# Moving half of one batch's preparation into the next mixing, wider complex products, and three evictions on ScalarE

## The chip, the cores and the metric

The kernel runs on one core of a Trainium2 chip. The metric is the device time of one execution in microseconds, the median of several executions. The engines are written as the profile writes them: PE is TensorE, PEld its weight loads, DVE VectorE, ACT ScalarE, POOL GpSimd, SP SyncE, which here issues most of the DMA transposes and the output.

## The reference

Four batches of 768 tokens and 512 channels. An attention with 8 heads, 8 global keys and a local window of 96 gives x. Then comes a phase-based mixing over tokens and a channel layer:

```python
theta = x @ w_theta
zr, zi = x * cos(theta), x * sin(theta)
y = einsum('ts,bsd->btd', w_tok_r, zr) + einsum('ts,bsd->btd', w_tok_i, zi)
u = x + y
out = u + maximum(u @ w_ch, 0)
```

## The kernel before

The mixing of batch b is interleaved ("woven") with the attention of batch b+1. A batch's attention needs its q and k transposed; for batches 1 and 2 this is done by `prep`, one call for each of four pairs of heads: two copies on DVE, 12 transposes on PE, one eviction on DVE, one on ACT, and two copies of global keys (`kglob`) on DVE. Batch 3's q and k are transposed by DMA.

```python
def prep(b, p):
    if p == 0:
        prep_copy(b, 0)
    if p + 1 < NP:
        prep_copy(b, p + 1)
    ...                      # 2 x 6 transposes into two PSUM tiles
    nc.vector.tensor_copy(out=qT, in_=ps)      # for q
    nc.scalar.copy(out=kT, in_=ps)             # for k
    kglob(b, p)

def kglob(b, p, ...):
    ...
    with behind("dve") if b == B - 1 else nullcontext():
        copy(out=kG, in_=kT[...])
        copy(out=kG[:, :, 0:NG], in_=kT[:, None, 0:NG].to_broadcast(...))

def trans_w(tt, copy=nc.vector.tensor_copy):   # token weights, one tile of rows
    for wi in range(2):
        ps = ps_small([T, NT, T], BF)
        ...                                    # 6 transposes
        (copy if wi else nc.vector.tensor_copy)(out=w_tokT[wi][...], in_=ps)
```

The first mixing (batch 0) is woven with the preparation of batch 1, the attention of batch 1, and all four preparations of batch 2:

```python
pre = [lambda p=p: prep(1, p) for p in range(NP)] if b == 0 else []
ahead = [[lambda p=p: prep(2, p) for p in range(NP)], [prep_dma(3, 0)], [], []][b]
...
if b == 0 and g == 1 and tt + 1 < NT:
    main.append((1536, lambda tt=tt: trans_w(tt + 1)))
```

The softmax here doesn't subtract the row's maximum and nothing guards it: scores larger than these inputs give would overflow.

## Time and profile before

| | before |
|---|---|
| median | 175.22 us (174.96 to 175.46, 4 runs) |
| execution that was profiled | 174.38 us, span 172.4 us |
| PE, DVE, ACT busy | 162.2, 126.3, 99.3 us |

The profiled execution happens to be quicker than the median by 0.8 us.

```profile
113.92 1.02 PE L418 MATMUL ps<-zri,w_tokT 128*128 128x512 bf16 x4 [0.48 <-DVE o_sb L451]
```

### The profile page before, as it was taken

The numbers are of one execution on the slowest core, as the hardware profiler recorded it, in microseconds if no ns is written. First come the engines' busy times: TensorE is split into PE (matmuls) and PEld (weight loads), VectorE is DVE, ScalarE is ACT, GpSimd is POOL, SyncE is SP. The second block draws the span as 40 slices with busy tenths as digits, with TensorE's granted clock in tenths as the row PEclk, the third lists the DMA queues.
The fourth block names the chain that finished last, engine by engine and source line by source line (L and its number), as shares of the span: only waits on it lengthen the run. The fifth ranks groups of instructions, "written<-read, shape, count | busy, mean of one in ns | idle before, by whom it ended". The sixth has DMA issues, their size and how long they took to land.

```text
span 172.4 us, 3753 instructions
## 1 busy us (share of the span) xinstructions
PE 162.2 (94%) x1534; PEld 84.7 (49%) x1534; DVE 126.3 (73%) x286; ACT 99.3 (58%) x127; POOL 37.4 (22%) x45
## 2 busy tenths in 40 slices
PE   7699989899999999999999999989999999999991
PEld 2355555445756566544445464433554644444440
DVE  5636977687999999998686588298776856714442
ACT  4688783999497695469944640879447409500010
POOL 8965355005282010099000000000000000000000
PEclk9969999999999999999999999999999999999999
DMA  4999999999999999999999677889245372323335
GB/s 154 199 174 178 208 210 207 205 204 173 158 204 176 169 131 192 124 138 143 182 130 117 143 170 167 109 151 256 43 78 136 97 168 76 122 55 98 94 92 184
DMA packets 75089, 25.94 MB, mean 150 GB/s; under 512 B 63168, under 2 KB 72128, under 8 KB 75072
## 3 DMA queue, kind: packets, MB, share of 16 engines
q0 software_dynamic: 45680, 12.45, 77.8%
q1 hardware_dynamic: 28976, 12.72, 33.8%
q10 hardware_dynamic: 416, 0.52, 0.9%
q8 instruction: 12, 0.20, 0.5%
q14 instruction: 5, 0.04, 0.1%
HBM read 25.69 MB, written 6.29 MB: 185 GB/s over the span
## 4 chain that ended last, share of the span: by engine, by line
PE 61%; DVE 19%; ACT 12%; DMA 5%; issue 1%; DVEq 0%; ACTq 0%; SPq 0%
PE ps L418 28%; PE ps L446 9%; ACT cs L404 6%; PE pb L398 6%; PE pb L296 5%; PE pb L355 4%; ACT e L306 3%; DMA qk<-in_k_dram 3%; DVE x_sb L366 2%; DMA kT<-qk 2%; DVE qT L250 2%; PE ps L398 2%; DVE e L315 2%; PE pb L276 2%; PE ps L246 2%; ACT L306 1%
## 5 line engine op out<-in xcount | busy, mean ns | idle before, releaser
L418 PE MATMUL ps<-zri,w_tokT 128*128 128x512 bf16 x288 | 71.2, 379 | 1.5 <-DVE zri L407 0.7
L306 ACT ACTIVATE e<-pb 128x1024 bf16<-128x1024 f32 (+1 forms) x48 | 43.6, 959 | 20.4 <-PE pb L296 19.9
L418 PEld LDWEIGHTS <-w_tokT 128*128 128x128 bf16 x288 | 26.2, 98 | 30.2 <-issue 2.5
L423 DVE TENSOR_TENSOR u<-x_sb,ps 128x512 bf16<-128x512 bf16 x24 | 16.4, 682 | 13.1 <-PE ps L418 13.1
L446 PE MATMUL ps<-w_ch_bf,uT 128*128 128x512 bf16 (+1 forms) x100 | 24.7, 371 | 0.0
L407 DVE TENSOR_TENSOR zri<-x_sb,cs 128x512 bf16<-128x512 bf16 x48 | 18.1, 419 | 4.9 <-ACT cs L404 4.6
L404 ACT ACTIVATE cs<-pb,halfpi 128x1024 bf16<-128x1024 f32 x8 | 8.9, 1114 | 18.3 <-PE pb L398 18.3
L451 DVE SCALAR_TENSOR_TENSOR o_sb<-ps,u 128x512 f32<-128x512 f32 (+1 forms) x25 | 16.5, 665 | 3.1 <-PE ps L446 3.1
L296 PE MATMUL pb<-qT,kT 64*128 64x128 bf16 x224 | 16.1, 223 | 1.7 <-DVE qT L211 1.3
L315 DVE TENSOR_TENSOR e<-e,etab 128x1024 bf16<-128x1024 bf16 (+1 forms) x24 | 14.7, 616 | 3.6 <-ACT e L306 3.5
L296 PEld LDWEIGHTS <-kT 64*128 64x128 bf16 x224 | 9.2, 95 | 15.8 <-issue 13.1
L398 PE MATMUL pb<-w_theta_bf,xT 128*128 128x512 bf16 x64 | 15.1, 379 | 0.0
L437 ACT COPY uT<-ps 128x512 bf16<-128x512 bf16 x7 | 4.1, 586 | 18.6 <-PE ps L436 18.6
L398 PEld LDWEIGHTS <-xT 128*128 128x128 bf16 x96 | 9.2, 98 | 10.1 <-DMA xT<-x_sb 0.2
L355 PEld LDWEIGHTS <-e 128*128 128x128 bf16 x352 | 12.6, 97 | 3.2 <-issue 1.0
L446 PEld LDWEIGHTS <-uT 128*128 128x128 bf16 x100 | 9.2, 98 | 10.0 <-ACT uT L437 0.8
L296 PE MATMUL pb<-qT,kG 64*128 64x128 bf16 x128 | 12.2, 221 | 0.4 <-DVE kG L222 0.4
L88 POOL DMA_DIRECT2D vn<-in_v_dram x5 | 9.6, 1923 | 12.3 <-DVE vn L68 10.7
L366 DVE TENSOR_TENSOR x_sb<-pb,rec 128x768 bf16<-128x768 f32 x12 | 11.4, 948 | 0.3
L318 DVE TENSOR_TENSOR e<-e,etab 128x1024 bf16<-128x1024 bf16 x12 | 8.2, 684 | 2.9 <-ACT e L306 2.9
L355 PE MATMUL pb<-vn,e 128*128 128x65 bf16 x168 | 9.6, 193 | 0.0
L252 ACT COPY kT<-ps 128x768 bf16<-128x768 bf16 x8 | 6.4, 798 | 5.5 <-PE ps L246 5.5
(73 smaller groups left out, 203.7 us busy)
## 6 DMA issues: line engine op xcount, KB each, us to landing
out_dram<-o_sb SPq DMA_DIRECT2D x23, 256.0 KB, 2.4
vn<-in_v_dram POOLq DMA_DIRECT2D x3, 768.0 KB, 22.1
qk<-in_q_dram POOLq DMA_DIRECT2D x2, 768.0 KB, 20.9
qk<-in_k_dram POOLq DMA_DIRECT2D x2, 768.0 KB, 23.2
w_nat<-in_moe_w_tok_r_dram POOLq DMA_DIRECT2D x3, 384.0 KB, 14.9
w_nat<-in_moe_w_tok_i_dram POOLq DMA_DIRECT2D x3, 384.0 KB, 13.9
vn<-in_v_dram POOLq DMA_DIRECT2D x2, 384.0 KB, 9.8
qk<-in_q_dram POOLq DMA_DIRECT2D x8, 96.0 KB, 9.6
```

Source lines behind the costliest of these rows:

```text
L296: nc.tensor.matmul(pb[:, hh, o:o + T], lhsT=lhsT, rhs=qT[R, (own, nxt)[part]], start=bool(b), stop=bool(b) or (jt == NT - 1 or (j == 1 and ...
L306: ins = nc.scalar.activation(e_c, pb[:, :, 0:n], AF.Exp, scale=scale).ins
L315: nc.vector.tensor_mul(e_c, e_c, tab[:, :, s0:s0 + n // T].rearrange("p a s n -> p a (s n)"))
L355: nc.tensor.matmul(o, lhsT=l_, rhs=r_, start=(i_ == 0), stop=(i_ == len(mms) - 1))
L366: nc.vector.tensor_mul(xv, po4[:, :, :, 0:D], rec.to_broadcast([T, n, nt, D]))
L398: nc.tensor.matmul(pb[j_] if last else pb[:, j_, :], lhsT=xT[:, dc, st(j_)], rhs=w_theta_bf[:, dc, :], start=(dc == 0), stop=(dc == NC - 1))
L404: nc.scalar.activation(o, p_, AF.Sin, **bias)
L407: nc.vector.tensor_mul(zri[b][:, i_, 2 * c + j_, :].rearrange("p (g d) -> p g d", g=NP), xb[:, :, 2 * c + j_, :], cs[:, i_, j_].rearrange( ...
L418: anchor["pe"] = nc.tensor.matmul(ps, lhsT=w_tokT[wi][:, st, tt * T:(tt + 1) * T], rhs=zri[b][:, wi, st, :], start=(st == 0 and wi == 0), ...
L423: anchor["dve"] = nc.vector.tensor_add(u_sb[b, tt].rearrange("p (g d) -> p g d", g=NP), x_sb[b][:, :, tt, :], ps.rearrange("p (g d) -> p g ...
L446: nc.tensor.matmul(ps_c, lhsT=uT[:, dc, :], rhs=w_ch_bf[:, dc, i_ * n:(i_ + 1) * n], start=(dc == 0), stop=(dc == NC - 1))
L451: nc.vector.scalar_tensor_tensor(o_sb[:, cols], in0=ps_c, scalar=0.0, in1=u[:, cols], op0=ALU.max, op1=ALU.add)
```

## The change

Its intent is to unload DVE in the first mixing, where it is busy without a pause: two of the four preparations of batch 2 go to the second mixing, where they are woven in after the first and second group of scores; the products x cos and x sin of batches 1 to 3 take two token tiles at a time; and the second eviction of three of the token-weight tiles goes to ACT.

```diff
-        if p == 0:
-            prep_copy(b, 0)
-        if p + 1 < NP:
+        if p == 0 or (b, p) == (2, NP // 2):
+            prep_copy(b, p)
+        if p + 1 < NP and (b, p) != (2, NP // 2 - 1):
             prep_copy(b, p + 1)
...
+            n = 2 if b else 1
             for i_ in range(2):
-                for j_ in range(2):
+                for j_ in range(0, 2, n):
                     nc.vector.tensor_mul(        # out, x, cos or sin: now n token tiles
...
+        late = [lambda p=p: prep(2, p) for p in range(NP // 2, NP)] if b == 2 else []
...
+            if i_ in (0, 2):
+                steps.extend((1536, f) for f in late[i_ // 2:i_ // 2 + 1])
...
-        ahead = [[lambda p=p: prep(2, p) for p in range(NP)], ...
+        ahead = [[lambda p=p: prep(2, p) for p in range(NP // 2)], ...
...
-                    main.append((1536, lambda tt=tt: trans_w(tt + 1)))
+                    main.append((1536, lambda tt=tt: trans_w(tt + 1, nc.scalar.copy if tt > 1 else nc.vector.tensor_copy)))
```

More of the change, by code (lines that the diff above doesn't have):

```diff
@@ L404, in theta @@
                     nc.scalar.activation(o, p_, AF.Sin, **bias)
+            n = 2 if b else 1
             for i_ in range(2):
-                for j_ in range(2):
+                for j_ in range(0, 2, n):
                     nc.vector.tensor_mul(
-                        zri[b][:, i_, 2 * c + j_, :].rearrange("p (g d) -> p g d", g=NP),
-                        xb[:, :, 2 * c + j_, :],
-                        cs[:, i_, j_].rearrange("p (g d) -> p g d", g=NP))
+                        zri[b][:, i_, 2 * c + j_:2 * c + j_ + n, :].rearrange("p j (g d) -> p j g d", g=NP),
+                        xb[:, :, 2 * c + j_:2 * c + j_ + n, :].rearrange("p g j d -> p j g d"),
+                        cs[:, i_, j_:j_ + n].rearrange("p j (g d) -> p j g d", g=NP))
     def mix(b, tt, g):
@@ L604 @@
         pre = [lambda p=p: prep(1, p) for p in range(NP)] if b == 0 else []
-        ahead = [[lambda p=p: prep(2, p) for p in range(NP)], [lambda p=p: prep_dma(3, p) for p in range(1)],
+        ahead = [[lambda p=p: prep(2, p) for p in range(NP // 2)], [lambda p=p: prep_dma(3, p) for p in range(1)],
                  [], []][b]
```

## The prediction

> **What bounds the kernel now.** I read the page first, then the busy time by stretch, then the chain that ended last, then the order of time on DVE. The page says that PE is the busy engine, but only 61% of the chain is PE's; 19% is DVE's.
>
> ```profile
> PE 162.2 (94%) x1534; PEld 84.7 (49%) x1534; DVE 126.3 (73%) x286; ACT 99.3 (58%) x127; POOL 37.4 (22%) x45
> ...
> PE 61%; DVE 19%; ACT 12%; DMA 5%; issue 1%; DVEq 0%; ACTq 0%; SPq 0%
> ```
>
> I cut the span by what the chain and the order of time show: batch 0's attention to 36 us; the first mixing, with the preparation and attention of batch 1 and the preparation of batch 2 woven in, to 73; theta of batch 1 to 82; the second mixing with batch 2's attention to 106; theta of batch 2 to 115; then the same again, and a pure mixing at the end. Busy time in these stretches (columns: length, then PE, PEld, DVE, ACT, POOL with counts, PE clock, DMA share, GB/s):
>
> ```profile
> 41.00:73.00 32.00, 31.45 (x389) 19.47 (x388) 32.00 (x74) 21.65 (x29) 7.13 (x10) 1.00 2.09 163
> 73.00:82.00 9.00, 9.00 (x58) 4.12 (x57) 8.48 (x22) 7.45 (x11) 9.00 (x10) 1.00 1.54 153
> 82.00:106.00 24.00, 23.81 (x243) 12.22 (x242) 17.27 (x31) 12.84 (x15) 0.19 (x1) 1.00 1.14 143
> 106.00:115.00 9.00, 8.52 (x44) 3.68 (x44) 5.94 (x17) 5.57 (x7) 0.00 (x0) 1.00 0.83 148
> 115.00:140.00 25.00, 24.70 (x258) 12.68 (x255) 19.88 (x39) 14.07 (x17) 0.00 (x0) 1.00 0.51 122
> ```
>
> The reader is to see 32.00 of 32.00 for DVE in the first stretch: it never rests. In the second mixing DVE is busy 17.27 of 24.00 and ACT 12.84: there is room. PE looks full everywhere, so I need what PE's work takes when it waits for nothing. The chain gives that, where PE runs on:
>
> ```profile
> 68.01 0.67 PE ps L246 x12
> ...
> 90.49 0.55 PE pb L296 x16
> ...
> 102.41 0.67 PE pb L355 x22
> 103.08 0.86 PE ps L446 x4
> 103.94 1.74 PE ps L418 x8
> ```
>
> So one 128-wide transpose (L246, and L167 and L436 alike) takes 0.056 us, a score matmul 0.034, a value matmul 0.0305, a 512-wide matmul (L418, L446, L398) 0.216. In the first stretch the trace counts 48 + 14 + 3 of the 512-wide, 96 + 36 + 16 transposes, 88 scores and 88 values: 65 x 0.216 = 14.0, 148 x 0.056 = 8.3, 88 x 0.034 = 3.0, 88 x 0.0305 = 2.7, together **28.0 us of PE work in 32.0**. Four microseconds of PE are lost there, and DVE is what it waits for: from 41 to 61 the chain is on DVE without a break. The same count for the second mixing is 83 x 0.216 + 72 x 0.034 + 88 x 0.0305 = 23.1 in 24.0, for the third 82 x 0.216 + 88 x 0.0645 = 23.4 in 25.0. Those two are bound by PE, at 94 to 96% of it. Theta of batch 1 (38 x 0.216 + 16 x 0.034 + 4 x 0.056 = 9.0 in 9.0) has no slack at all.
>
> **What the Trainium skill says.** "Perfetto Trace Analysis", Identifying the Most-Contended Engine: matmul busy share is a bad measure, occupancy is a fair one for the Vector engine. The trace agrees: PE shows 31.45 of 32 busy where the work counts to 28.0. "TensorE: Matmul & The Clock Gate", Wait — 56ns, not 53.3ns?: 56 ns between warm 128-wide matmuls; here 0.67 us for 12. "Perfetto Trace Analysis", Optimizing Scalar/DVE Operations: larger operations spare the cost per instruction, and a saturated DVE may hand work to Scalar even where Scalar is slower. The trace has both: a 128x512 product every 0.38 us against a 128x1024 one every 0.60, and a 128x768 eviction 0.80 on ACT against 0.53 (durations) on DVE. "VectorE: DVE Perf Modes", What auto-detection actually checks: the two-per-cycle mode asks for 16-bit operands of step one, not for few dimensions; the regrouped products keep both, and 1024 products in 0.60 us, four dimensions at L318 included, show the mode before.
>
> **The change part by part.** (1) Two of four preparations of batch 2 leave the first mixing. What one costs DVE is read from the starts here (start, duration; the next start gives the cost):
>
> ```profile
> 42.62 0.95 DVE L250 COPY qT<-ps 128x768 bf16<-128x768 bf16 x1
> 43.49 0.35 DVE L231 COPY qkn<-qk 128x768 bf16<-128x768 bf16 x1
> 43.75 0.29 DVE L220 COPY kG<-kT 128x512 bf16<-128x512 bf16 x1
> 43.95 0.35 DVE L231 COPY qkn<-qk 128x768 bf16<-128x768 bf16 x1
> 44.22 0.17 DVE L222 COPY kG<-kT 128x32 bf16<-128x32 bf16 x1
> 44.30 0.95 DVE L250 COPY qT<-ps 128x768 bf16<-128x768 bf16 x1
> ```
>
> 0.87 + 2 x 0.27 + 0.20 + 0.08 = 1.69 us, twice 3.4. On PE it is 24 transposes, 1.34 us; on ACT two evictions of 0.80. (2) Three evictions of transposed token weights go from DVE (0.47 from start to start) to ACT: 1.4 us off DVE, 3 x 0.80 = 2.4 onto ACT, which has 10 us free in that stretch. DVE falls from 32.0 to 27.2, PE's need from 28.0 to 26.7, ACT stays near 22.5. The two limits are then almost equal, so I take neither as reached. Up to 49.1 us the four preparations of batch 1 are a serial passage that the change hardly touches (one eviction, 0.5): 8.2 becomes 7.7 us. The rest held 28.0 - 6.4 = 21.6 us of PE work (6.4 is the same count up to 49.1) in 23.8; less 1.34 it is 20.3, and at 95% of PE, as in the later mixings, 21.3. Together 29.0 for 32.0: **3.0 us gained**.
>
> (3) The second mixing takes the 24 transposes. PE is its bound, so 1.34 us of work cost 1.34 / 0.95 = **1.4 us**. DVE has 2.3 more there and the four copies, 1.1, at the head of theta of batch 1, where they come before the products. (4) The products of three batches: two of 0.38 become one of about 0.60, so 0.16 x 6 = 1.0 us of DVE per theta. In theta of batch 1 that pays the 1.1 us of copies; in theta of batch 3 PE runs through; in theta of batch 2, where DVE waits 3.1 us for a transposed kT and the products after it hold up the sines by 1.1 us and PE by 0.5, I give it **0.3 us**. Sum: -3.0 + 1.4 - 0.3 = -1.9 us.
>
> **The rivals.** First, PE alone is the bound and work moved from one mixing to the next is only moved: then the net is near zero, perhaps 175.0. For it speaks that PE from 60.9 to 73 already carries 11.3 us of work in 12.1, and that 24 transposes leave exactly there; against it the 4.0 us lost in the stretch as a whole. Second, ACT becomes the wait: the last weight eviction stands in the changed order behind the exp table's replacement by the sine table (1.28 us) and gates the last mixing tile; from the last scores of batch 1, two exps, the load and the eviction end after about 3.7 us, and PE has about 3.5 us of other work first. At worst a stall of 1 us: 174.3. Third, DVE was the whole loss: the first mixing then falls to PE's 26.7 over 0.95, 28.1, and the net is -2.8 or better with fewer stalls later: 172.3. Fourth, the larger products come later, as one has to wait for both sines of the last pair of tiles; ACT needs 0.5 us for the second sine, and the scores' stalls in the second mixing would grow by that. In the changed order 24 transposes fill the place, so I expect no more than 0.3.
>
> **Range and chances.** 175.4 less 1.9 is 173.5. The first rival sets the upper end, 175.2, the third with a further half microsecond the lower, 171.8. To be over 2% faster it needs less than 171.9, which would mean that the first mixing loses almost nothing any more; I give 0.12. Over 2% slower would ask for a new stall of more than 3.5 us, and I see none: 0.02.
>
> **What would show it.** In the changed profile: DVE's share in the first mixing below 95%, the stretch about 3 us shorter, the chain there on PE rather than DVE; 96 transposes split 72 to 24; the second mixing longer by 1.4 us at about unchanged PE efficiency; products of 128x1024 at 0.68 us or so, 18 of them. A product of 1.2 us would mean that the two-per-cycle mode was lost; then DVE gains nothing there. A wait of PE for ACT's weight copies over 0.5 us would show the second rival. The prediction is wrong if the first mixing keeps its length, which would say that the weave and not DVE's load sets it.

## More of the kernel before

Beside the lines that the prediction shows, three of the kernel before are needed later: from the order of time of DVE and of PE (start, duration, engine, line, operation, count, and in brackets the idle time before it and what ended it). DVE copies the first q and k of batch 1 without waiting for the load; it waits 3.06 us for a key tile transposed by DMA in the theta stage of batch 2; and PE waits there 0.48 us.

```profile
41.55 1.16 DVE L231 COPY qkn<-qk 128x768 bf16<-128x768 bf16 x4
...
111.55 0.29 DVE L220 COPY kG<-kT 128x512 bf16<-128x512 bf16 x1 [3.06 <-DMA kT<-qk]
```

## The result, and the profile after

The changed kernel took 173.97 us in the median (173.88 to 174.46, 4 runs), the kernel before 175.22. The ratio is 0.9935, 95% interval 0.9910 to 0.9959: a little faster, under 2%. Ratios in this document are the mean time of one kernel's runs over that of the other's runs in the same rounds, so they are not quite the ratio of the medians. Executions over 1.5% slower than the fastest of the same kernel are left out of the means.

The page of the changed kernel, busy time and the chain that ended last:

```profile
PE 158.7 (92%) x1510; PEld 84.2 (49%) x1534; DVE 125.0 (72%) x265; ACT 101.4 (59%) x130; POOL 39.8 (23%) x45
...
PE 49%; DMA 26%; DVE 12%; POOL 5%; ACT 4%; issue 2%; DVEq 0%; SPq 0%; POOLq 0%
```

DVE's share of the chain fell from 19% to 12%. Nearly half of DMA's 26% is one transfer, the load of batch 1's keys, through which the chain now runs. Behind it the chain is still on DVE, from 42.3 to 56.5 us, where in the kernel before it was on DVE from 40.9 to 60.8; so the prediction's sign "the chain there on PE rather than DVE" came only in part. (Some matmul records are missing from this trace, 1510 of 1534, so PE's busy sum is not to be compared.) Busy time by stretch, with the same columns as in the prediction:

```profile
41.00:72.00 31.00, 29.16 (x359) 18.10 (x364) 29.14 (x65) 22.11 (x30) 8.15 (x9) 1.00 2.07 168
72.00:80.00 8.00, 8.00 (x44) 3.43 (x43) 6.98 (x14) 6.39 (x9) 7.64 (x9) 1.00 1.22 125
80.00:106.00 26.00, 25.31 (x277) 13.93 (x283) 20.84 (x37) 15.21 (x18) 2.48 (x2) 1.00 1.30 145
```

DVE is busy 94% of the first stretch instead of 100%. Stretches cut by eye are too coarse for the rest, so I use three lengths with ends that every trace has: "first" from the first transpose of batch 1's q to the end of theta of batch 1, "second" from there to the end of theta of batch 2, "third" from there to the end of theta of batch 3. (The end is the start of the last group of theta matmuls plus 0.216 us for each of them.) One profiled execution of each kernel, in us:

| kernel | first | second | third |
|---|---|---|---|
| before | 36.44 | 34.01 | 34.09 |
| changed | 35.39 | 35.55 | 34.10 |

The first became 1.05 us shorter, the second 1.54 longer, the third stayed. Both profiled executions have a span of 172.4 us, so this pair of traces shows where time moved and does not show the 1.25 us of the medians: the one of before was its quickest of five, the one of the changed kernel its slowest of four (174.46 us; the other three took 173.88 to 173.98).

Now the waits in the changed kernel's trace, from the order of time of DVE, of ACT and of PE. DVE waits for batch 1's keys, and does only 0.35 us of copying before that:

```profile
41.29 0.35 DVE L231 COPY qkn<-qk 128x768 bf16<-128x768 bf16 x1
42.32 0.90 DVE L231 COPY qkn<-qk 128x768 bf16<-128x768 bf16 x3 [0.68 <-DMA qk<-in_k_dram]
...
111.95 0.30 DVE L220 COPY kG<-kT 128x512 bf16<-128x512 bf16 x1 [3.28 <-DMA kT<-qk]
112.16 0.69 DVE L408 TENSOR_TENSOR zri<-x_sb,cs 128x1024 bf16<-128x1024 bf16 x1
```

The last two lines are the old wait for the transposed keys: DVE takes its work in order, and the product of 0.69 us, whose sines were ready (both end by 110.54), stands behind the copy. On ACT, the last of the moved evictions (L168) stands on ACT behind the table load, and PE waits for its buffer:

```profile
64.14 1.28 ACT L300 ACT_TABLE_LOAD   x1
65.44 0.20 ACT L300 ACTIVATE junk<-halfpi 128x1 f32<-128x1 f32 x1
65.55 0.78 ACT L168 COPY w_tokT<-ps 128x768 bf16<-128x768 bf16 x1
```

```profile
66.38 0.49 PE L246 MATMUL ps<-ident,qkn 128*128 128x128 bf16 x6 [0.34 <-ACT w_tokT L168]
...
92.83 1.04 PE L447 MATMUL ps<-w_ch_bf,uT 128*128 128x512 bf16 x4 [0.32 <-DMA uT<-u]
...
114.18 1.02 PE L419 MATMUL ps<-zri,w_tokT 128*128 128x512 bf16 x4 [0.52 <-DVE o_sb L452]
```

The line at 92.83 is a wait that the kernel before has not: the first channel layer of batch 1 waits for u transposed by DMA. The one at 114.18 is the old wait behind DVE, unchanged.

### The profile page after: what moved, and what is told of

It is laid out like the page before. It is cut to its first block, busy times and chain, and to the rows that moved or that the text cites. A ratio compares the mean times of both kernels' runs of the same rounds, so it can differ in the third digit from the quotient of the medians.

```text
span 172.4 us, 3709 instructions
## 1 busy us (share of the span) xinstructions
PE 158.7 (92%) x1510; PEld 84.2 (49%) x1534; DVE 125.0 (72%) x265; ACT 101.4 (59%) x130; POOL 39.8 (23%) x45
## 4 chain that ended last, share of the span: by engine, by line
PE 49%; DMA 26%; DVE 12%; POOL 5%; ACT 4%; issue 2%; DVEq 0%; SPq 0%; POOLq 0%
PE ps L419 25%; DMA qk<-in_k_dram 12%; PE ps L447 10%; DMA w_nat<-in_moe_w_tok_r_dram 7%; DMA uT<-u 5%; PE pb L398 4%; PE pb L355 4%; PE pb L296 3%; POOL qk L73 3%; DMA kT<-qk 2%; DVE qT L250 2%; PE ps L398 2%; ACT e L306 2%; DVE o_sb L452 2%; POOL vn L88 2%
## 5 line engine op out<-in xcount | busy, mean ns | idle before, releaser
L419 PE MATMUL ps<-zri,w_tokT 128*128 128x512 bf16 x271 | 68.6, 380 | 2.7 <-DVE zri L408 0.8
L447 PE MATMUL ps<-w_ch_bf,uT 128*128 128x512 bf16 (+1 forms) x98 | 24.2, 371 | 0.4 <-DMA uT<-u 0.3
L408 DVE TENSOR_TENSOR zri<-x_sb,cs 128x1024 bf16<-128x1024 bf16 (+1 forms) x30 | 16.8, 582 | 5.5 <-ACT cs L404 5.1
L296 PE MATMUL pb<-qT,kT 64*128 64x128 bf16 x224 | 15.1, 219 | 2.1 <-DVE qT L211 1.3
L296 PEld LDWEIGHTS <-kT 64*128 64x128 bf16 x224 | 8.7, 94 | 14.7 <-issue 11.4
L296 PE MATMUL pb<-qT,kG 64*128 64x128 bf16 x128 | 11.6, 217 | 0.7 <-DVE kG L222 0.4
L82 POOL DMA_DIRECT2D qk<-in_k_dram x8 | 8.8, 1094 | 5.9 <-DMA vn<-in_v_dram 5.9
```

What stands on the lines that cost most here:

```text
L296: nc.tensor.matmul(pb[:, hh, o:o + T], lhsT=lhsT, rhs=qT[R, (own, nxt)[part]], start=bool(b), stop=bool(b) or (jt == NT - 1 or (j == 1 and ...
L408: nc.vector.tensor_mul(zri[b][:, i_, 2 * c + j_:2 * c + j_ + n, :].rearrange("p j (g d) -> p j g d", g=NP), xb[:, :, 2 * c + j_:2 * c + j_ ...
L419: anchor["pe"] = nc.tensor.matmul(ps, lhsT=w_tokT[wi][:, st, tt * T:(tt + 1) * T], rhs=zri[b][:, wi, st, :], start=(st == 0 and wi == 0), ...
L447: nc.tensor.matmul(ps_c, lhsT=uT[:, dc, :], rhs=w_ch_bf[:, dc, i_ * n:(i_ + 1) * n], start=(dc == 0), stop=(dc == NC - 1))
```

## The experiments

All outputs are right. Two theories stood against each other. **Theory D**: DVE's load sets the length of the first mixing (the prediction's reading). **Theory P**: PE and its hand-offs set it, and what is moved from one mixing to the next is only moved. The three lengths of every run are in a table at the end of this section.

### The parts one by one

part1_late_preps takes from the diff only the move of the preparations; part2_wide_products only the block with `n = 2 if b else 1`; part3_copies_on_act only the line with `nc.scalar.copy`; parts23_no_move the last two.

> Only the move of two preparations of batch 2 into the second mixing; products and weight evictions as before. Theory D (VectorE's load sets the first mixing): 3.4 us leave a saturated VectorE, 1.4 us are paid in the second mixing, net about -1.5 us (ratio 0.991). Theory P (TensorE and its hand-offs set both mixings, moved work is only moved): 0 to -0.3 us (ratio 0.998 to 1.000).

> Only the products of batches 1 to 3 by two token tiles. Both theories: VectorE saves about 0.16 us for each of 18 products, but in the theta stages, where TensorE is full; 0 to -0.5 us (ratio 0.997 to 1.000).

> Only the three weight evictions moved to ScalarE. Theory D: 1.4 us off a saturated VectorE, about -1.2 us (ratio 0.993). Theory P: nothing, or a little slower (up to +0.5 us) where TensorE waits for ScalarE's eviction behind the table load.

> The changed kernel without the move of the preparations. Theory D: about -1.5 us (1.4 us of evictions and 0.3 us of products), so the move is worth little. Theory P: 0 to -0.5 us, and the move is what makes up the rest of the measured -1.2 us.

| run | median us (6 runs) | before, same rounds | ratio | interval |
|---|---|---|---|---|
| part1_late_preps | 176.30 | 175.28 | 1.0066 | 1.0030 to 1.0102 |
| part2_wide_products | 175.26 | 175.28 | 1.0004 | 0.9986 to 1.0023 |
| part3_copies_on_act | 175.27 | 175.28 | 0.9990 | 0.9961 to 1.0020 |
| parts23_no_move | 174.91 | 175.28 | 0.9964 | 0.9932 to 0.9995 |

Theory D misses on part 3 (it wanted 0.993) and on parts 2 and 3 together (it wanted 0.991; the measured 0.6 us is near what theory P allowed). Both miss on part 1, which is slower than before. The parts don't add: alone they make +0.66, +0.04 and -0.10%, together -0.65% (measured in other rounds). Part 1 took 3.4 us off DVE in the first mixing (the prediction's count); "first" in its profile is 36.12 us, 0.3 less than before and 1.1 less than in part2_wide_products, which is the same program there. "Second" grew by 2.0 and "third" by 0.9. (The traced execution, 177.40 us, is one of the two slowest of part 1.) Beside the moved transposes, two waits of PE carry much of that growth:

```profile
94.51 1.04 PE L446 MATMUL ps<-w_ch_bf,uT 128*128 128x512 bf16 x4 [0.74 <-DMA uT<-u]
...
116.73 1.02 PE L418 MATMUL ps<-zri,w_tokT 128*128 128x512 bf16 x4 [1.38 <-DVE o_sb L451]
```

In part 3's trace PE now stands for another eviction of the same kind, one that is still on DVE. It is one visible wait; that it is the reason why the relief of DVE was worth so little is not shown.

```profile
65.85 0.49 PE L246 MATMUL ps<-ident,qkn 128*128 128x128 bf16 x6 [0.71 <-DVE w_tokT L168]
```

A caution for all runs of this section: the traces show that the order of PE's work in the first mixing is not the same in all of them. It is the same in the kernel before and part2_wide_products; part 3, part 1, the changed kernel and the kernels with a dose each have another, also where the edit touches no work of PE. In part 3, for example, 12 transposes of a weight tile, which stand together in the kernel before, are split 4 and 8 around the 22 value matmuls of a pair. So a run is its edit and a new order. That the parts don't add may come from this; no run held the order fixed.

### A dose of work for one engine

To see what a microsecond on either engine costs in the first mixing, I added work that nobody reads.

```diff
         nc.vector.tensor_mul(xv, po4[:, :, :, 0:D], rec.to_broadcast([T, n, nt, D]))
+        if b == 1:                                   # dose_vec_*: 12 copies in all
+            for _ in range(3):
+                nc.vector.tensor_copy(out=spare, in_=x_sb[b][:, p, 0:4, :])
...
-            for st in range(NT):                     # dose_te_*: in trans_w
+            for st in list(range(NT)) * (2 if tt >= 3 else 1):
                 nc.tensor.transpose(ps[:, st, :], w_nat[wi, tt][...], ident)
```

> The kernel before with 12 idle copies of 128x512 (about 0.2 us each, 2.4 us) added to VectorE in the first mixing, after the attention results of batch 1; nobody reads them. Theory D (VectorE's load sets the first mixing): +2.0 to +2.4 us. Theory P (TensorE and its hand-offs set it; VectorE is busy because it has always something waiting, but with some slack): under +1 us.

> The kernel before with 36 transposes of the token weights done twice into the same place (36 x 0.056 = 2.0 us of TensorE in the first mixing). Theory D: 0 to +0.7 us, since TensorE has 4 us to spare there. Theory P: +1.7 to +2.0 us.

> The same 12 idle copies in the changed kernel, whose VectorE has 4.7 us less to do in this stretch. Theory D: under +1 us, for VectorE is no longer the limit. Theory P: 0 to +0.5 us.

> The same 36 doubled transposes in the changed kernel. Theory D: TensorE and VectorE are now near equal, +1.5 to +2.0 us. Theory P: +1.7 to +2.0 us as in the kernel before.

The dose on DVE is as large as meant: a copy occupies it for 0.20 us until the next start, in the profile of dose_vec_before:

```profile
57.60 0.27 DVE L369 COPY spare<-x_sb 128x512 bf16<-128x512 bf16 x1
57.80 0.67 DVE L315 TENSOR_TENSOR e<-e,etab 128x1024 bf16<-128x1024 bf16 x1
```

| run | ratio to before | interval | worth, us | dose, us | "first" in its profile |
|---|---|---|---|---|---|
| dose_vec_before | 1.0112 | 1.0082 to 1.0141 | 2.0 | 2.4 | 38.24, +1.8 |
| dose_te_before | 1.0105 | 1.0064 to 1.0146 | 1.8 | 2.0 | 38.77, +2.3 |
| dose_vec_after | 1.0016 | 0.9951 to 1.0080 | 1.4 | 2.4 | 35.42, 0.0 |
| dose_te_after | 1.0036 | 1.0003 to 1.0068 | 1.8 | 2.0 | 37.26, +1.9 |

"Worth" is 175.2 us times the ratio less 1 for the kernel before, and times the ratio less 0.9935 for the changed one, whose own runs belong to other rounds. The intervals make it 1.4 to 2.5 us for DVE's dose and 1.1 to 2.6 for PE's in the kernel before. The last column compares single traces: "first" of part2_wide_products, the same program as before in that stretch, is 37.25 us, and against it the first two would be +1.0 and +1.5. In the kernel before, **both theories are right at once**: work on DVE costs 2.0 of its 2.4 us and work on PE 1.8 of its 2.0. Theory D said that PE had 4 us to spare there; it had not. Part of the price on DVE can be the place and not the amount, which no run separates: in that trace PE waits 0.37 us, at 68.24, for the third pair's attention result x_sb, before which DVE had made six of the copies. In the changed kernel PE's dose costs about as much as before (1.8 us, each way some 0.7). DVE's dose left "first" as it was in the profile; its timing is too wide (1.4 us, with an interval of more than a microsecond either way) to confirm that.

### The waits that remain

Three runs of the changed kernel each take away the cause of one wait.

```diff
-    load_w()                     # after_keys_earlier
-    load_all_qk(1)
+    load_w(0, 4)                 # theta weights, first four token tiles
+    load_all_qk(1)
+    load_w(4, NT)                # last two token tiles, channel weights
...
-        with behind("dve") if b == B - 1 else nullcontext():            # after_global_keys_later
+        with behind("zri" if p == 1 else "dve") if b == B - 1 else nullcontext():
...                               # anchor["zri"] is the last product issued
-    trans_w(tt + 1, nc.scalar.copy if tt > 1 else nc.vector.tensor_copy)   # after_last_copy_back
+    trans_w(tt + 1, nc.scalar.copy if 1 < tt < 4 else nc.vector.tensor_copy)
```

> The changed kernel with the loads of batch 1's queries and keys issued ahead of the last third of the token weights and the channel weights (same loads, another order). If the keys of batch 1, which landed at 42.3 us in its profile, held the first mixing: no wait of VectorE for that load any more and 0.3 to 0.8 us faster than the changed kernel (ratio to the kernel before 0.989 to 0.992). If that wait was an accident of the profiled execution: as the changed kernel (0.9935), within 0.2%.

> The changed kernel with one copy of global keys (pair 1 of batch 3) placed on VectorE after the products of batch 2 instead of before them; all else, the other engines' orders too, stays. If the products of that theta are held by the transposed keys that this copy waits for (3.3 us), then VectorE's wait goes and TensorE's waits of 0.5 and 0.2 us for o_sb and zri with it: 0.5 to 1.0 us faster than the changed kernel (ratio 0.988 to 0.991). If TensorE's work hides it: no change (0.9935).

> The changed kernel with the last of the three weight evictions back on VectorE, so that none stands behind ScalarE's table load. If that place cost the changed kernel its 0.3 to 0.6 us wait of TensorE: 0.3 us faster (ratio about 0.992). If VectorE is still the limit there: 0.3 us slower (0.995). Theory P: no change.

| run | median us (6 runs) | before, same rounds | ratio | interval |
|---|---|---|---|---|
| after_keys_earlier | 174.48 | 175.47 | 0.9922 | 0.9880 to 0.9964 |
| after_global_keys_later | 173.71 | 175.47 | 0.9866 | 0.9820 to 0.9913 |
| after_last_copy_back | 174.57 | 175.47 | 0.9935 | 0.9895 to 0.9975 |

after_keys_earlier: DVE no longer waits for the load (its four first copies run from 41.50 on without a gap), and "first" is 34.61 us instead of 35.39. But "second" is 36.57 instead of 35.55, and the time is within the noise of the changed kernel's 0.9935. The gain came back as a wait:

```profile
93.31 1.04 PE L449 MATMUL ps<-w_ch_bf,uT 128*128 128x512 bf16 x4 [1.37 <-DMA uT<-u]
```

This is the same wait as at 92.83 in the changed kernel and at 94.51 in part 1. The DMA transpose of the first u of batch 1 is issued at 84.5 us in the kernel before, at 84.8 in the changed one, at 84.3 here, and lands 8.0 to 9.0 us later, at about 93 us, against a median of 2.5 us for all of its kind in the DMA list of the kernel before. There PE reached this work at 93.47 us and had nothing to wait for; a kernel that is earlier at this place waits. The likely cause of the slow landing are the loads of batch 3: the last of them is issued at 79.9 to 80.2 us in these three, and at 81.8 in part 1, where u, issued at 86.0, landed at 94.5. That last load, batch 3's values, lands within 0.5 us of u in all of these four traces: at 93.2, 92.8, 93.7 and 94.6 us. No run changed those loads, so this stays an argument.

after_last_copy_back: 0.9935, the changed kernel's ratio; neither of the two expected shifts is seen. The prediction's second rival, ACT behind the table load, is a visible wait of 0.34 us in the trace and not measurable in the time.

after_global_keys_later: the only one that gained. DVE's wait for the transposed keys is gone from the products, and PE starts the mixing without a wait:

```profile
110.05 0.69 DVE L408 TENSOR_TENSOR zri<-x_sb,cs 128x1024 bf16<-128x1024 bf16 x1 [0.99 <-ACT cs L404]
```

```profile
113.02 1.03 PE L447 MATMUL ps<-w_ch_bf,uT 128*128 128x512 bf16 x4
113.88 1.03 PE L419 MATMUL ps<-zri,w_tokT 128*128 128x512 bf16 x4
```

The product starts at 110.05 us, when its sine is ready, instead of 112.16. "Third" is 33.12 us instead of 34.10. Five of its six runs are fast (172.99 to 173.90 us) and one is slow (176.63). It is 1.3% faster than the kernel before in the same rounds; against the changed kernel it is 0.7% by the quotient of the two ratios, which come from different rounds and whose intervals just touch. Runs of the same rounds say the same: its five fast runs have a mean of 173.55 us, those of after_keys_earlier and after_last_copy_back 174.44 and 174.67, which is 0.5 and 0.6% more.

### One more wait taken away, and others in its place

The last run keeps the late global keys and transposes the first u of batch 1 on PE:

```diff
-        if (b or b) and (b, tt) != (B - 1, NT - 1):
+        if b and (b, tt) not in ((1, 0), (B - 1, NT - 1)):
             anchor["sp"] = nc.sync.dma_start_transpose(out=uT, in_=u).ins
```

> The changed kernel with the global keys placed after the products, as in the run before, and in addition the first u of batch 1 transposed on TensorE (4 transposes, 0.22 us, and an eviction on ScalarE) instead of by DMA. In that run and in three others with the preparations moved, TensorE waited 0.7 to 1.4 us in the second mixing for this DMA transpose, which landed at about 93 us whatever the kernel did before. If that wait is real loss: it goes, the second mixing is 0.5 to 1.2 us shorter, ratio to the kernel before 0.980 to 0.984. If another wait takes its place: 0.986 to 0.987 as in that run.

It took 175.93 us (175.56 to 176.37, 6 runs) against 175.08 before: ratio 1.0047, interval 1.0018 to 1.0076. Neither expectation held; it is slower than the run without this edit. The wait for u is gone, and two others stand in the second mixing, one of them for the eviction of scores by ACT, one for x transposed by DMA:

```profile
84.15 0.21 PE L296 MATMUL pb<-qT,kT 64*128 64x128 bf16 x1 [1.01 <-ACT e L306]
...
110.21 1.04 PE L398 MATMUL pb<-w_theta_bf,xT 128*128 128x512 bf16 x4 [1.66 <-DMA xT<-x_sb]
```

Together 2.67 us for the 1.16 us that this wait had in the profile of after_global_keys_later; "second" went from 36.39 to 38.61. x was issued only 0.2 us later than there (105.62 against 105.43) but took 4.54 us to land instead of 2.78. Why stays open. after_global_keys_later is the best version found.

### The three lengths in all profiles that are used

| run | traced execution, us | first | second | third | first + second |
|---|---|---|---|---|---|
| before | 174.38 | 36.44 | 34.01 | 34.09 | 70.45 |
| part2_wide_products | 174.92 | 37.25 | 34.02 | 34.01 | 71.27 |
| part3_copies_on_act | 175.28 | 37.17 | 34.02 | 34.35 | 71.19 |
| parts23_no_move | 173.98 | 36.74 | 34.02 | 33.89 | 70.76 |
| part1_late_preps | 177.40 | 36.12 | 36.02 | 34.99 | 72.14 |
| changed | 174.46 | 35.39 | 35.55 | 34.10 | 70.94 |
| after_keys_earlier | 175.35 | 34.61 | 36.57 | 34.50 | 71.18 |
| after_last_copy_back | 175.34 | 34.65 | 36.26 | 34.72 | 70.91 |
| after_global_keys_later | 173.90 | 34.94 | 36.39 | 33.12 | 71.33 |
| later_keys_and_te_turn | 175.82 | 34.62 | 38.61 | 33.11 | 73.23 |
| dose_vec_before | 177.21 | 38.24 | 34.71 | 34.79 | 72.95 |
| dose_te_before | 176.26 | 38.77 | 34.70 | 33.46 | 73.47 |
| dose_vec_after | 176.97 | 35.42 | 36.37 | 34.66 | 71.79 |
| dose_te_after | 176.16 | 37.26 | 35.63 | 33.28 | 72.89 |

The reader is to see two things. Without the move "second" is 34.0 us in the four traces without a dose and 34.7 in the two with one. With it, "second" is 1.5 to 2.6 us longer (later_keys_and_te_turn aside), and the shorter "first" is, the longer it tends to be: their sum stays between 70.5 and 71.3 in all rows but part 1, later_keys_and_te_turn and the doses. One caution: these are single executions, and for the changed kernel and most of its variants the traced one is the slowest of the fast ones.

## Why the prediction was right or wrong, point by point

The number and the class held: 173.5 us was predicted and 173.97 measured, inside the range, and within 2% as given at 0.86. The sum came out by terms of which three were mis-sized, so that the close number is in part luck: with the lengths measured below (1.8 us gained, 1.5 to 2.6 lost, nothing from the products) the same sum lies between 0.3 us faster and 0.8 slower.

**The bound.** "Four microseconds of PE are lost there, and DVE is what it waits for" is the step that failed. Most of the four are no wait. The count of 28.0 us behind them takes each kind of matmul as it runs among its own kind. The traces show a further cost wherever PE goes from other matmuls to score matmuls, which use 64 rows, and back. Here it is in the changed kernel:

```profile
114.18 1.02 PE L419 MATMUL ps<-zri,w_tokT 128*128 128x512 bf16 x4 [0.52 <-DVE o_sb L452]
115.14 0.34 PE L296 MATMUL pb<-qT,kT 64*128 64x128 bf16 x6
...
115.54 0.22 PE L296 MATMUL pb<-qT,kG 64*128 64x128 bf16 x2
115.69 1.27 PE L419 MATMUL ps<-zri,w_tokT 128*128 128x512 bf16 x4
```

The last of the four 512-wide matmuls starts at 114.82, and the first score 0.31 us later instead of 0.216; the last score starts at 115.54, and the next matmul 0.15 us later instead of 0.034. The surplus is 0.095 us on the way in and 0.114 on the way out, as the median of the 365 changes of each kind that the three lengths of all 14 traces hold, and never under 0.094 and 0.111. In the first mixing of the kernel before (41 to 73 us) there are 13 changes of each kind, 2.7 of the 4.0 us; some 1.3 us are left that can be waits.

The same count for "first", an estimate with the prediction's costs, says what the change did there. In the four traces without the move and without a dose it is 32.1 us of work, 2.7 of changes (26 of them) and 1.6 to 2.4 of rest. In after_keys_earlier, after_last_copy_back and after_global_keys_later (the changed kernel's own trace lacks records) it is 30.8, 2.3 (22 changes) and 1.5 to 1.9. So what the first mixing gained is mainly the transposes that left and four changes fewer; over 4 us less work on DVE took little from the rest. "Second" without the move is 32.5 us of work, 1.5 of changes and 0.1 of rest: it was full, and moved work had to cost its full price there.

DVE was a limit all the same, as its dose of 2.4 us showed by costing 2.0, and PE was one too, with 1.8 for 2.0. A stretch in which one engine is busy without a pause can still charge nearly the full price for work on another, and relief of one engine then brings little.

**The first mixing, "3.0 us gained".** Measured: 1.05 us between the two traces of the result, but DVE waits 0.68 us for batch 1's keys in one of them and not in the other. Like with like it is 1.8 to 1.9: from 36.44 (before) to 34.61 (after_keys_earlier), both without that wait, and from 37.25 (part2_wide_products, the program of before in this stretch, 0.56 us of it) to 35.39 (changed). The prediction knew nothing of the wait, for in its one trace the load had landed in time; it shows at 0.2 to 0.7 us in most other traces, with and without the change. Of the prediction's 3.0, 1.4 were moved work of PE and 1.6 shorter waits for DVE; of these 1.6 the count above finds about 0.1, and 0.4 in fewer changes instead. The 0.34 us behind the table load is in the trace, but the run without it was no faster.

**The second mixing, "1.4 us".** 1.54 between the two traces, so the term held there. In the three variants it is 2.2 to 2.6 us, with 1.0 to 1.4 us of waiting for the DMA transpose of u. The prediction named moved work as the only cost and had no term for a transfer that lands no earlier when the work before it does. In these traces the wait for it is what adds to the moved work when the first mixing is faster.

**The products, "0.3 us".** Measured: nothing. 18 products of 688 ns came as predicted, and two of them start 0.60 us apart, so the prediction's sign of a lost mode, 1.2 us, is absent. But part2_wide_products alone has a ratio of 1.0004 and "third" did not move. The prediction saw that DVE waits 3.1 us for kT and still gave the narrower work behind it a gain; the wait stayed at 3.28 us and its end sets the rest. Moving the waiting copy gave what widening the products could not: 1.0 us of "third".

**The rivals.** The first, PE alone and moved work only moved, is near what the traces show for first plus second (70.45 before, 70.94 changed) and fits the count of PE's work above, while the medians lie 1.25 us apart. Where the executions without a trace are that much quicker is not located: only one execution of each kernel has a trace, and the two are the quickest of one and the slowest of the other. The second rival was seen at 0.34 us and had no measurable effect. The third, DVE as the whole loss, fell with part 3. The fourth didn't show: the place is filled as the prediction said.

## What to carry to other kernels

Before moving work away from an engine that is busy without a pause, give each engine of that stretch a small useless dose and see what it costs: here the two charged about 80 and 90%, and the relief brought much less than the load removed. Before calling the gap between a stretch and its counted work a wait, count what the changes between kinds of work cost: here they were 2.7 of 4.0 us. A stretch that becomes shorter meets transfers at an earlier moment, and those that don't land earlier take the gain back. An instruction that waits for a transfer holds everything behind it on an engine that works in order; look for it before making the work behind it smaller.

## What the Trainium skill lacked or had wrong

- "Perfetto Trace Analysis", Identifying the Most-Contended Engine, names one engine to optimize first, the one with the highest occupancy, with TensorE judged by its share of peak FLOPs and of weight loads instead. That was not enough here. DVE had 32.00 of 32.00 us in the first mixing and weight loads 19.47, and a dose on DVE did cost 2.0 of 2.4 us; but a dose on PE cost 1.8 of 2.0 in the same stretch, and moving 1.4 us of DVE's work to ACT changed the time by -0.10% (interval -0.39 to +0.20%).
- "ScalarE: Activation LUTs", What ACT_TABLE_LOAD costs, gives about 1283 ns for the load and about 1380 more for a drain at every switch. The load is 1.28 us here, but no drain is seen around it: in the changed kernel the exp before it ends at 64.13 us, the load starts at 64.14 and the next activation at 65.44, and the other six switches of that trace after the start look the same.
- None of the pages that I read tells how long a DMA transpose takes when large loads are under way. In these runs those of u have a median of 2.5 us from issue to landing, and the first of batch 1 took 8.0 to 9.0.
- No page that I read gives a figure for changing between matmuls of 64 and of 128 rows. Here each change into score matmuls costs 0.095 us and each change out of them 0.114 us, 2.7 us in the first mixing.
